# First transposed weight block made on TensorE, first gate product split, in a fused GELU MLP forward and backward kernel

## The chip, the cores and the metric

The kernel runs on one core of a Trainium2 chip. The metric is the device time of one execution in microseconds. Before the change it is 275.32 us, the median of three runs (275.23, 275.32, 275.83). The profile shown is one more execution, of 275.51 us; the span from its first to its last instruction is 273.7 us, and TensorE's granted clock was 1.0.

A core has five engines that run their own instruction streams side by side: TensorE (PE; PEld is its weight load), VectorE (DVE), ScalarE (ACT), GpSimd (POOL) and SyncE (SP). Transfers between HBM and on-chip memory are issued on the queues of SP, ACT and POOL. Matrix products write to PSUM, in eight banks of 128 x 512 f32.

## The reference

An MLP with a tanh-approximated GELU, and its gradients, with S = 2048 rows, D = 448, F = 1792, all in bf16:

```python
def _fwd_reference(x, w1, b1, w2, b2):
    h = jnp.einsum("bsd,df->bsf", x, w1) + b1
    h = _gelu(h)
    return jnp.einsum("bsf,fd->bsd", h, w2) + b2

_out, _vjp = jax.vjp(_f, x, w1, b1, w2, b2)
_grads = _vjp(grad_out)      # for x, w1, b1, w2, b2
```

With u = x w1 + b1 and h = gelu(u), the kernel must give out = h w2 + b2, and from q = grad_out w2^T and gh = gelu'(u) * q the five gradients: gh w1^T, x^T gh, the column sums of gh, h^T grad_out and the column sums of grad_out.

## The kernel before, in words

Everything is held transposed: u, h, q and gh have the feature dimension F on the partitions, 128 at a time. S is cut into 4 blocks of 512 rows and F into 7 pairs of 128-row tiles, which makes 28 steps `g`, one block after the other. One step computes, for a pair of F tiles and a block of 512 rows:

- u (`M1` and `rest`, L239 and L249): 6 products over full 128 rows of D and 2 over the last 64, into one double-bank PSUM tile `u`.
- q (`M4` and `rest`, L258 and L252): the same number, into the double-bank tile `q`. Their stationary operand is `w2T_sb`, w2 transposed.
- On ACT (`act_first`): u to `V` with its bias (L285, twice), its square `A` (L286) and h by the GELU table (L287); later the tanh (L357).
- On DVE: the cubic (L354), the slope (L361 to L364) and the gate (L375), which multiplies the slope with q and writes gh. `V`, `A` and the cubic have one buffer each, `u` and `q` one PSUM tile each.
- Beside it TensorE runs "pieces" (L406): single products of 448 columns that add up earlier h tiles times w2 (out, kind "o") or earlier gh tiles times w1^T (kind "g"). A unit of 14 pieces has one of the four banks of `psum_a`, which are handed out in turn.

The order on every engine is the order in which the program is written; nothing reorders it. Each step `g` writes the remainder of u of the next step, q of its own, the gate, the ACT chain of the next step, the pieces, and M1 of the step after the next.

The start is written out by hand, because the inputs arrive piece by piece. The loads go on SP's queue in the order of L189 to L218 (three small ones on ACT's). x, grad_out and w2 are loaded with a transposing DMA (`load_x`, `load_g`, `load_w2T`), 256 or 512 rows at a time; w1, and w2's rows for the pieces (`load_w2`), with plain ones. The first step is cut into two halves of 256 rows, `r`:

- `keep_warm` (L279): products whose result nobody reads, eight at first on zeros, later on loaded data.
- `first_products` (L297, L300): u of step 0. Its halves go to two banks of `psum_a` and to a tile of the pool that holds `q`.
- `first_chain` (L311 to L336): on each half the ACT and DVE chain up to the finished slope.
- `M1(1)` and `rest(1, None)`: u of step 1.
- Three products of `keep_warm`, then `first_q` (L271): q of step 0, by halves in one double-bank tile, eight products a half, with one more of `keep_warm` between. It reads rows 0 to 256 of `w2T_sb`, and both halves of grad_out's first block.
- In the loop, `dve_gate(0)` (L371): two gates, one for each half; then the pieces of step 0, two products for each of four out units.

After the 28 steps the remaining pieces run, then the gradients of w1 (L569, L577) and of w2 (L588). Two sums over the partitions are made on POOL (L544, L555).

Of the kernel before, what the change touches and what calls it, by code (L numbers as in the profile page):

```python
# [7 lines left out]

# [10 lines left out]
def kernel(  # L19
# [15 lines left out]
    nc = tc.nc  # L35
# [29 lines left out]
    psum_g = ctx.enter_context(tc.tile_pool(name="psum_g", bufs=1, space=bass.MemoryType.PSUM))  # L65
    psum_a = ctx.enter_context(tc.tile_pool(name="psum_a", bufs=4, space=bass.MemoryType.PSUM))

# [120 lines left out]
    nc.vector.memset(w128[:], 1.0 / P)  # L188
    load_x(0, 0, HB)  # L189
# [4 lines left out]
    nc.scalar.activation(out=T_flat[0:1, SB + 2:SB + 3], in_=ones, func=ACT.Gelu_apprx_tanh)  # L194
    load_w1(nc.sync, 256, 512)
    load_g(0, 0, HB)
    load_w2T(0, 256)
    load_g(0, HB, SB)
    load_w2(0, 2)
# [61 lines left out]
    def first_q():  # L261


        q = psum_g.tile([P, 2, SB], F32, name="q")
        g_of[0] = q
        for r in range(2):
            rs = slice(r * HB, (r + 1) * HB)
            for kt in (KF, *range(KF)):
                ps = slice(0, DL if kt == KF else P)
                for h in range(2):  # L270
                    nc.tensor.matmul(q[:, r, h * HB:(h + 1) * HB], lhsT=w2T_sb[ps, kt, cols(0, h)], rhs=gq(0)[ps, kt, rs],  # L271
                                     start=(kt == KF and h == 0), stop=(kt == KF - 1),
                                     tile_position=(0, 0) if kt == KF else None, skip_group_check=True)
            if r == 0:
                keep_warm(1, w1_sb[:, 1, 0:P], xq(0)[:, 1, :])
# [13 lines left out]
    def first_products():  # L289

        ub = psum_g.tile([P, 2, SB], F32, name="q")
        u_of[0] = [[psum_a.tile([P, SB], F32, name="acc")[:, 0:HB] for h in range(2)], [ub[:, h, 0:HB] for h in range(2)]]
        for r in range(2):
# [8 lines left out]
            if r == 0:  # L302
                keep_warm(1, warm[:, 0:P], warm)

    def first_chain():
# [27 lines left out]

        def times(r):
# [7 lines left out]
        copy(1)  # L342
        square(1)
        tanh(0)
        gelu(1)
        slope(0)
# [4 lines left out]
        times(1)  # L351

# [13 lines left out]
    def dve_gate(g):  # L366
        q = g_of.pop(g)
        if g == 0:
            for r in range(2):
                rs = slice(r * HB, (r + 1) * HB)  # L370
                nc.vector.scalar_tensor_tensor(out=ghT(g)[:, :, rs], in0=t_of(g)[:, :, rs], scalar=1.0,  # L371
                                               in1=q[:, r, :].rearrange("p (h s) -> p h s", h=2),
                                               op0=ALU.add, op1=ALU.mult)
        else:
# [253 lines left out]
```

## Time and profile before

| what | value |
|---|---|
| median of three runs | 275.32 us |
| the profiled execution | 275.51 us |
| its span | 273.7 us |
| TensorE busy | 267.9 us (98%) |
| DVE busy | 191.1 us (70%) |
| ACT busy | 144.1 us (53%) |
| POOL busy | 53.5 us (20%) |
| from 0 to 7.4 us: PE, DVE, ACT busy | 5.89, 2.16, 2.80 us |
| from 7.4 to 14.3 us | 6.38, 5.80, 6.01 us |
| from 14.3 to 48.4 us | 33.53, 33.24, 28.36 us |
| from 48.4 to 270 us | 221.59, 149.90, 106.42 us |

A row such as `13.14 1.28 DVE L371 ... x2 [0.77 <-PE q L271]` gives the start and the duration in us, the engine, the line of the kernel, and in brackets how long the engine stood idle before it and what ended that. In the chain of work, each piece is what the next one waited for; SPq is the issue of transfers on SP's queue. Rows of the form `c <- a, b` name the tile that is written and the ones that are read: `w2T_g` is w2 transposed, `w_gw` is w2's rows, `w_x` is w1, `xg_h` holds x and grad_out transposed.

### The profile page before, as it was taken

The numbers are of one execution on the slowest core, as the hardware profiler recorded it, in microseconds if no ns is written. First come the engines' busy times: TensorE is split into PE (matmuls) and PEld (weight loads), VectorE is DVE, ScalarE is ACT, GpSimd is POOL, SyncE is SP. The second block draws the span as 40 slices with busy tenths as digits, with TensorE's granted clock in tenths as the row PEclk, the third lists the DMA queues.
The fourth block names the chain that finished last, engine by engine and source line by source line (L and its number), as shares of the span: only waits on it lengthen the run. The fifth ranks groups of instructions, "written<-read, shape, count | busy, mean of one in ns | idle before, by whom it ended". The sixth has DMA issues, their size and how long they took to land.

```text
span 273.7 us, 3611 instructions
## 1 busy us (share of the span) xinstructions
PE 267.9 (98%) x1407; PEld 124.7 (46%) x1407; DVE 191.1 (70%) x229; ACT 144.1 (53%) x191; POOL 53.5 (20%) x59
## 2 busy tenths in 40 slices
PE   7999999999999999999999999999999999999995
PEld 3444434444444344444444445554445555555552
DVE  2799999999999999999888871149999970000000
ACT  3968879788988778887777740011111221112111
POOL 0000002830301503033031137111700029300000
PEclk9999999999999999999999999999999999999999
DMA  7999999999579927255534339999999931101111
GB/s 158 197 278 236 153 208 180 305 155 315 125 169 220 251 58 149 37 154 124 137 111 79 110 103 217 273 359 243 174 235 244 240 101 57 44 9 50 50 51 36
DMA packets 101533, 43.78 MB, mean 160 GB/s; under 512 B 90092, under 2 KB 98156, under 8 KB 101516
## 3 DMA queue, kind: packets, MB, share of 16 engines
q1 hardware_dynamic: 94432, 26.91, 52.8%
q0 software_dynamic: 4512, 14.69, 17.1%
q10 hardware_dynamic: 2572, 1.95, 2.3%
q8 instruction: 11, 0.18, 0.3%
q14 instruction: 6, 0.05, 0.1%
HBM read 7.00 MB, written 14.23 MB: 78 GB/s over the span
## 4 chain that ended last, share of the span: by engine, by line
PE 82%; DVE 12%; SPq 2%; DMA 2%; ACT 0%; issue 0%; DVEq 0%
PE acc L406 27%; PE acc L588 16%; PE acc L569 13%; PE q L258 10%; PE u L239 9%; PE u L249 4%; DVE T L361 3%; DVE Bt L354 3%; DVE ghT_h L375 3%; PE acc L577 2%; DMA w2T_g<-in_w_dram 2%; DVE T L364 2%; SPq L145 1%; DVE T L362 1%; PE q L271 1%; DVE T L363 1%
## 5 line engine op out<-in xcount | busy, mean ns | idle before, releaser
L406 PE MATMUL acc<-w_gw,hT_h 128*128 128x448 bf16 x224 | 46.3, 353 | 0.0
L406 PE MATMUL acc<-w1T_gw,ghT_h 128*128 128x448 bf16 x224 | 45.1, 353 | 0.0
L285 ACT ACTIVATE VA<-u,b_col 128x512 f32<-128x512 f32 x54 | 33.9, 679 | 13.3 <-PE u L249 13.3
L239 PE MATMUL u<-xg_h,w_x 128*128 128x512 bf16 x162 | 39.4, 379 | 0.7 <-ACT VA L285 0.6
L258 PE MATMUL q<-xg_h,w2T_g 128*128 128x512 bf16 x162 | 39.7, 381 | 0.0
L375 DVE SCALAR_TENSOR_TENSOR ghT_h<-T,q 128x1024 bf16<-128x1024 bf16 x27 | 33.0, 1220 | 7.9 <-PE q L258 6.6
L569 PE MATMUL acc<-gh_nat,w_x 128*128 128x512 bf16 (+1 forms) x192 | 36.7, 353 | 0.0
L357 ACT ACTIVATE T<-Bt 128x1024 bf16<-128x1024 f32 x27 | 28.5, 1057 | 14.6 <-DVE Bt L354 14.5
L361 DVE SCALAR_TENSOR_TENSOR T<-VA,hT_h 128x1024 bf16<-128x1024 f32 x27 | 33.1, 1227 | 0.0
L354 DVE SCALAR_TENSOR_TENSOR Bt<-VA 128x1024 f32<-128x1024 f32 x27 | 32.9, 1219 | 0.0
L406 PEld LDWEIGHTS <-hT_h 128*128 128x128 bf16 x224 | 21.9, 98 | 21.4
L406 PEld LDWEIGHTS <-ghT_h 128*128 128x128 bf16 x224 | 21.9, 98 | 20.9
L554 DVE TENSOR_TENSOR VA<-VA,gh_nat 128x1792 f32<-128x1792 f32 x14 | 30.0, 2142 | 0.5
L286 ACT ACTIVATE VA<-VA 128x1024 f32<-128x1024 f32 x27 | 28.5, 1057 | 0.9
L287 ACT ACTIVATE hT_h<-VA 128x1024 bf16<-128x1024 f32 x27 | 28.1, 1040 | 0.0
L569 PEld LDWEIGHTS <-w_x 128*128 128x128 bf16 x192 | 18.7, 98 | 17.8 <-issue 0.4
L258 PEld LDWEIGHTS <-w2T_g 128*128 128x128 bf16 x162 | 13.6, 97 | 24.2 <-issue 11.4
L239 PEld LDWEIGHTS <-w_x 128*128 128x128 bf16 x162 | 15.8, 98 | 18.7 <-issue 0.8
L590 ACT CAST w_gw<-acc 128x448 bf16<-128x448 f32 x13 | 6.9, 532 | 32.6 <-PE acc L588 32.6
L571 ACT CAST w1T_gw<-acc 128x512 bf16<-128x512 f32 (+1 forms) x12 | 6.3, 532 | 30.1 <-PE acc L569 27.4
L379 POOL DMA_DIRECT2D hT_dram<-hT_h x28 | 20.4, 729 | 0.1
L420 ACT CAST io_g<-acc 128x448 bf16<-128x448 f32 x16 | 8.3, 520 | 22.6 <-PE acc L406 22.6
(74 smaller groups left out, 241.0 us busy)
## 6 DMA issues: line engine op xcount, KB each, us to landing
hT_dram<-hT_h POOLq DMA_DIRECT2D x28, 256.0 KB, 4.2
out_dram<-io_o POOLq DMA_DIRECT2D x8, 224.0 KB, 4.3
out_dram<-io_g POOLq DMA_DIRECT2D x8, 224.0 KB, 3.4
w_x<-in_x_dram POOLq DMA_DIRECT2D x1, 1344.0 KB, 10.9
w2T_g<-in_grad_out_dram POOLq DMA_DIRECT2D x1, 1344.0 KB, 14.2
out_dram<-w_gw SPq DMA_DIRECT2D x4, 336.0 KB, 2.4
w_x<-in_w_dram SPq DMA_DIRECT2D x2, 384.0 KB, 4.5
out_dram<-w1T_gw ACTq DMA_DIRECT2D x2, 384.0 KB, 4.3
```

The lines of the kernel that those rows point to most:

```text
L239: nc.tensor.matmul(u_of[g][h], lhsT=w1_sb[:, 1 + kt, cols(g, h)], rhs=xq(g // NPAIR)[:, 1 + kt, :], start=(kt == 0), stop=False, skip_grou ...
L258: nc.tensor.matmul(g_of[g][:, h, :], lhsT=w2T_sb[:, kt, cols(g, h)], rhs=gq(g // NPAIR)[:, kt, :], start=False, stop=(kt == KF - 1), skip_ ...
L285: nc.scalar.activation(out=V_of(g)[:, h, :], in_=u[h], func=ACT.Identity, bias=b1_col[:, ft:ft + 1])
L286: nc.scalar.activation(out=A_of(g), in_=V_of(g), func=ACT.Square, scale=math.sqrt(3.0 * GELU_C * GELU_A))
L354: nc.vector.scalar_tensor_tensor(out=B_of(g), in0=A_of(g), scalar=3.0 * GELU_C, in1=V_of(g), op0=ALU.add, op1=ALU.mult)
L357: nc.scalar.activation(out=t_of(g), in_=B_of(g), func=ACT.Tanh, scale=-1.0 / 3.0)
L361: nc.vector.scalar_tensor_tensor(out=p_of(g), in0=A_of(g), scalar=GELU_C, in1=hT(g), op0=ALU.add, op1=ALU.mult)
L375: nc.vector.scalar_tensor_tensor(out=ghT(g), in0=t_of(g), scalar=1.0, in1=q[:], op0=ALU.add, op1=ALU.mult)
L406: nc.tensor.matmul(self.ps[:, 0:D], lhsT=lhsT, rhs=rhs, start=(ft == 0), stop=(ft == NF - 1 and not bias))
L554: nc.vector.tensor_tensor(out=gsb_v, in0=gsb_v, in1=gh_rows(st, 0, NF), op=ALU.add)
L569: nc.tensor.matmul(psv, lhsT=x_all[:, st, kt * P:(kt + 1) * P], rhs=gh_rows(st, a0, a1), start=(st == 0), stop=(st == NS - 1))
L588: nc.tensor.matmul(ps[:, 0:D], lhsT=h_blk[ft][:, st, :], rhs=g_all[:, st, :], start=(st == 0), stop=(st == NS - 1))
```

## The change

- w2's first 256 rows are no longer loaded with a transposing DMA for `w2T_sb`. Their plain load, `load_w2(0, 2)`, which served only the pieces, moves up on SP's queue: from behind grad_out's two halves to directly behind x's, ahead of w1's second part.
- An identity of 128 x 128 is made on POOL (`make_identity`: a clear and an `affine_select`, before which the compiled program loads code for POOL; a further code load stands, as before the change, ahead of the sum at L544).
- `turn_w2`: eight products of w2's rows with the identity, each 128 columns, into two banks, behind `first_products` and ahead of `M1(1)`. `turned(i)`: two ACT copies of 128 x 512 from PSUM into `w2T_sb`, one behind ACT's copy of half 1, one behind half 1's GELU, within `first_chain`.
- u's second half and q of step 0 have tiles of one bank for each half (`psum_h`), in a pool that is closed after the start, and whose banks `q` of the later steps takes over.
- `first_q` runs in two parts: blocks 0 and 1 of D for both halves, then four of the pieces of step 0 (two each of the first two out units), then blocks 2 and 3. Both gates stand behind it. The other four pieces of step 0 remain where they were.
- The four products of `keep_warm` around `first_q` are gone.
- `first_chain` stands behind `M1(1)` and `rest(1, None)` in the text; on ACT and DVE its order changes only by the two copies.

```diff
@@ -5,6 +5,7 @@
 import concourse.tile as tile
 from concourse import bass_isa, bass_utils, mybir
 from concourse._compat import with_exitstack
+from concourse.masks import make_identity
 
 ACT = mybir.ActivationFunctionType
 ALU = mybir.AluOpType
@@ -62,8 +63,10 @@
     iop = ctx.enter_context(tc.tile_pool(name="iop", bufs=2))
     dram = ctx.enter_context(tc.tile_pool(name="dram", bufs=1, space=bass.MemoryType.DRAM))
     psum_u = ctx.enter_context(tc.tile_pool(name="psum_u", bufs=1, space=bass.MemoryType.PSUM))
-    psum_g = ctx.enter_context(tc.tile_pool(name="psum_g", bufs=1, space=bass.MemoryType.PSUM))
     psum_a = ctx.enter_context(tc.tile_pool(name="psum_a", bufs=4, space=bass.MemoryType.PSUM))
+
+    first = ExitStack()
+    psum_h = first.enter_context(tc.tile_pool(name="psum_h", bufs=1, space=bass.MemoryType.PSUM))
 
     hT_dram = dram.tile([F, S], BF16, name="hT_dram")
     hT_dram_v = hT_dram.rearrange("(ft p) s -> p ft s", p=P)
@@ -186,17 +189,18 @@
     nc.vector.memset(ones, 1.0)
     nc.vector.memset(b1_rows, 0.0)
     nc.vector.memset(w128[:], 1.0 / P)
+    ident = T_flat[:, 6 * SB:6 * SB + P]
+    make_identity(nc, ident)
     load_x(0, 0, HB)
     load_x(0, HB, SB)
     nc.scalar.dma_start(out=w1_sb[:, 1:KD, 0:256], in_=w1[DL:D, 0:256].rearrange("(k p) f -> p k f", p=P))
     nc.scalar.dma_start(out=b1_rows[0:NF, :], in_=b1.rearrange("(t p) -> t p", p=P))
     nc.scalar.dma_start(out=w1_sb[DL:P, 0, 0:256], in_=w1[0:DL, 0:256])
     nc.scalar.activation(out=T_flat[0:1, SB + 2:SB + 3], in_=ones, func=ACT.Gelu_apprx_tanh)
+    load_w2(0, 2)
     load_w1(nc.sync, 256, 512)
     load_g(0, 0, HB)
-    load_w2T(0, 256)
     load_g(0, HB, SB)
-    load_w2(0, 2)
     load_w1(nc.sync, 512, 768)
     load_w2T(256, 512)
     load_w2(2, 4)
@@ -258,21 +262,20 @@
                 nc.tensor.matmul(g_of[g][:, h, :], lhsT=w2T_sb[:, kt, cols(g, h)], rhs=gq(g // NPAIR)[:, kt, :],
                                  start=False, stop=(kt == KF - 1), skip_group_check=True)
 
-    def first_q():
-
-
-        q = psum_g.tile([P, 2, SB], F32, name="q")
-        g_of[0] = q
+    def first_q(kts):
+
+
         for r in range(2):
             rs = slice(r * HB, (r + 1) * HB)
-            for kt in (KF, *range(KF)):
+            if kts[0] == 0:
+                g_of.setdefault(0, []).append(psum_h.tile([P, SB], F32, name="h%d" % r))
+            q = g_of[0][r]
+            for kt in kts:
                 ps = slice(0, DL if kt == KF else P)
                 for h in range(2):
-                    nc.tensor.matmul(q[:, r, h * HB:(h + 1) * HB], lhsT=w2T_sb[ps, kt, cols(0, h)], rhs=gq(0)[ps, kt, rs],
-                                     start=(kt == KF and h == 0), stop=(kt == KF - 1),
+                    nc.tensor.matmul(q[:, h * HB:(h + 1) * HB], lhsT=w2T_sb[ps, kt, cols(0, h)], rhs=gq(0)[ps, kt, rs],
+                                     start=(kt == 0 and h == 0), stop=(kt == KF),
                                      tile_position=(0, 0) if kt == KF else None, skip_group_check=True)
-            if r == 0:
-                keep_warm(1, w1_sb[:, 1, 0:P], xq(0)[:, 1, :])
 
     def keep_warm(n, weights, moving):
         for i in range(n):
@@ -288,8 +291,7 @@
 
     def first_products():
 
-        ub = psum_g.tile([P, 2, SB], F32, name="q")
-        u_of[0] = [[psum_a.tile([P, SB], F32, name="acc")[:, 0:HB] for h in range(2)], [ub[:, h, 0:HB] for h in range(2)]]
+        u_of[0] = [[t[:, 0:HB] for t in ua], [psum_h.tile([P, SB], F32, name="h%d" % h)[:, 0:HB] for h in range(2)]]
         for r in range(2):
             rs = slice(r * HB, (r + 1) * HB)
             for h in range(2):
@@ -302,6 +304,18 @@
             if r == 0:
                 keep_warm(1, warm[:, 0:P], warm)
 
+    def turn_w2():
+
+        for kt in range(KD):
+            n = DL if kt == KF else P
+            for h in range(2):
+                o = (2 * (kt % 2) + h) * P
+                nc.tensor.matmul((ta, pw)[kt // 2][0:n, o:o + P], lhsT=w2_sb[:, h, kt * P:kt * P + n], rhs=ident,
+                                 start=True, stop=True)
+
+    def turned(i):
+        nc.scalar.copy(out=w2T_sb[:, 2 * i:2 * i + 2, 0:2 * P], in_=(ta, pw)[i].rearrange("p (k f) -> p k f", k=2))
+
     def first_chain():
 
         V, A, Bt, t, p, h0 = V_of(0), A_of(0), B_of(0), t_of(0), p_of(0), hT(0)
@@ -330,6 +344,10 @@
             nc.vector.scalar_tensor_tensor(out=p[:, :, R[r]], in0=A[:, :, R[r]], scalar=GELU_C, in1=h0[:, :, R[r]],
                                            op0=ALU.add, op1=ALU.mult)
             nc.vector.tensor_scalar(out=p[:, :, R[r]], in0=p[:, :, R[r]], scalar1=-0.5, scalar2=None, op0=ALU.add)
+
+        def gate(r):
+            nc.vector.scalar_tensor_tensor(out=ghT(0)[:, :, R[r]], in0=t[:, :, R[r]], scalar=1.0,
+                                           in1=g_of[0][r].rearrange("p (h s) -> p h s", h=2), op0=ALU.add, op1=ALU.mult)
 
         def times(r):
             nc.vector.tensor_scalar(out=t[:, :, R[r]], in0=t[:, :, R[r]], scalar1=1.0, scalar2=None, op0=ALU.add)
@@ -340,15 +358,22 @@
         gelu(0)
         cubic(0)
         copy(1)
+        turned(0)
         square(1)
         tanh(0)
         gelu(1)
+        turned(1)
         slope(0)
         cubic(1)
         tanh(1)
         times(0)
         slope(1)
         times(1)
+        first_q((0, 1))
+        run_pieces([U["o", 0, j] for j in (0, 0, 1, 1)])
+        first_q((2, KF))
+        gate(0)
+        gate(1)
 
     def dve_first(g):
         nc.vector.scalar_tensor_tensor(out=B_of(g), in0=A_of(g), scalar=3.0 * GELU_C, in1=V_of(g), op0=ALU.add, op1=ALU.mult)
@@ -365,14 +390,7 @@
 
     def dve_gate(g):
         q = g_of.pop(g)
-        if g == 0:
-            for r in range(2):
-                rs = slice(r * HB, (r + 1) * HB)
-                nc.vector.scalar_tensor_tensor(out=ghT(g)[:, :, rs], in0=t_of(g)[:, :, rs], scalar=1.0,
-                                               in1=q[:, r, :].rearrange("p (h s) -> p h s", h=2),
-                                               op0=ALU.add, op1=ALU.mult)
-        else:
-            nc.vector.scalar_tensor_tensor(out=ghT(g), in0=t_of(g), scalar=1.0, in1=q[:], op0=ALU.add, op1=ALU.mult)
+        nc.vector.scalar_tensor_tensor(out=ghT(g), in0=t_of(g), scalar=1.0, in1=q[:], op0=ALU.add, op1=ALU.mult)
 
     def store_h(g):
         b, c = blk(g)
@@ -457,6 +475,8 @@
             turns.setdefault(at, []).append((b, c0, c1))
     stored = 0
 
+    ua = [psum_a.tile([P, SB], F32, name="acc") for _ in range(2)]
+    ta = psum_a.tile([P, SB], F32, name="acc")
     pw = psum_a.tile([P, SB], F32, name="acc")
     keep_warm(8, warm[:, 0:P], warm)
 
@@ -464,24 +484,25 @@
         nc.vector.transpose(out=b1_turned[32 * i:32 * (i + 1), :], in_=b1_rows[:, 32 * i:32 * (i + 1)])
     nc.vector.tensor_copy(out=b1_col[:], in_=b1_turned[:, 0:NF])
     first_products()
-    first_chain()
+    turn_w2()
     M1(1)
     rest(1, None)
-
-    keep_warm(3, w1_sb[:, 1, 0:P], xq(0)[:, 1, :])
-    first_q()
+    first_chain()
+    first.close()
+    psum_g = ctx.enter_context(tc.tile_pool(name="psum_g", bufs=1, space=bass.MemoryType.PSUM))
     for g in range(NSTEP):
         b, c = blk(g)
         pieces = [U[k] for k in seq[b] for _ in range(NF)]
         n = len(pieces)
         own = pieces[n * c // NPAIR:n * (c + 1) // NPAIR]
-        grown = [U[k] for k in grow[b] for _ in range(2)]
+        grown = [U[k] for k in (grow[b] if g > 0 else grow[b][2:]) for _ in range(2)]
         nxt = g + 1 if g + 1 < NSTEP else None
         if g > 0:
             rest(nxt, g)
             M4(g)
         flush(False)
-        dve_gate(g)
+        if g > 0:
+            dve_gate(g)
         if nxt is not None:
             act_first(nxt)
         flush(True)
```

The helper that is called, outside the kernel:

```python
def make_identity(nc, identity, nomemset=False):
    sq1, sq2 = identity.shape
    ...
    nc.gpsimd.memset(identity, 0.0)
    nc.gpsimd.affine_select(out=identity, in_=identity, compare_op=mybir.AluOpType.not_equal,
                            fill=1.0, base=0, pattern=[[-1, sq]], channel_multiplier=1)
```

## The prediction

> **What bounds the kernel now.** I read the page first, then the chain that ended last in order of time, then the start instruction by instruction. The page says that TensorE is busy nearly everywhere, and that DVE still holds an eighth of the chain.
>
> ```profile
> PE 267.9 (98%) x1407; PEld 124.7 (46%) x1407; DVE 191.1 (70%) x229; ACT 144.1 (53%) x191; POOL 53.5 (20%) x59
> ...
> PE 82%; DVE 12%; SPq 2%; DMA 2%; ACT 0%; issue 0%; DVEq 0%
> ```
>
> The chain in order of time says where DVE's share lies (start, duration, what):
>
> ```profile
> 4.80 1.30 SPq L145
> 6.15 4.46 DMA w2T_g<-in_w_dram
> 10.65 1.15 PE q L271 x8
> 12.02 1.10 PE q L271 x8
> 13.14 1.28 DVE ghT_h L371 x2
> 14.42 1.14 DVE Bt L354
> ...
> 47.25 0.43 DVE T L362
> 47.69 0.68 ACT VA L285
> 48.41 1.46 PE u L239 x6
> ```
>
> From 6.15 the end waits for w2's first transposed load (landed 10.61), then for the two halves of the first q, then for DVE. DVE repeats one step every 5.07 us (its L354 starts at 14.34, 19.42, 24.49, 29.56) against TensorE's 4.75 (L239 at 14.48, 19.23, 23.98), up to 47.7. At 48.41 TensorE, idle for 0.58 us before, takes the chain over and keeps it to the end. So a time saved before 14.34 on DVE is kept; a time saved on TensorE there is not.
>
> The start in the timeline (start, duration, engine, line):
>
> ```profile
> 7.37 1.47 PE L239 MATMUL u<-xg_h,w_x 128*128 128x512 bf16 x6
> ...
> 9.31 0.82 PE L279 MATMUL acc<-xg_h,w_x 128*128 128x512 bf16 x3
> ...
> 11.94 0.42 DVE L336 TENSOR_TENSOR T<-T 128x512 bf16<-128x512 bf16 x1
> ...
> 11.99 1.06 ACT L286 ACTIVATE VA<-VA 128x1024 f32<-128x1024 f32 x1
> ...
> 12.97 1.67 PE L406 MATMUL acc<-w_gw,hT_h 128*128 128x448 bf16 x8
> ...
> 13.14 1.28 DVE L371 SCALAR_TENSOR_TENSOR ghT_h<-T,q 128x512 bf16<-128x512 bf16 x2 [0.77 <-PE q L271]
> ...
> 14.34 1.22 DVE L354 SCALAR_TENSOR_TENSOR Bt<-VA 128x1024 f32<-128x1024 f32 x1
> ```
>
> DVE is ready for the first gate at 12.37 and waits 0.77 us for q, for both halves, since they are one tile. L354 also needs ACT's square L286 (ends 13.05). So 0.77 is nearly all that the edit can win.
>
> **SP's queue.** One transpose (1.30 us to issue) goes, and the 0.58 us load of w2's rows moves from 8.94 to 3.56, ahead of w1's second part. So w1's two loads issue at 4.19 and 4.82 (0.63 later), grad's halves at 5.43 (before 4.80) and 6.78 (before 7.49), and all behind them some 1.4 us sooner. With the latencies of the same loads from the DMA view: w2's rows, 3.56 plus 4.0 (their own) or 3.8 (w1's in that place): 7.4, up to 7.56. w1: 4.19 + 3.8 = 7.99, its remainder 4.82 + 3.4 = 8.22. Grad: 5.43 + 4.2 = 9.63 and 6.78 + 4.1 = 10.88, or 11.24 with the 4.46 of the slowest transpose there. The later loads covered themselves before and come sooner.
>
> **TensorE.** The first products end at about 7.3 as before. Eight products of 128 columns with the identity follow, which no row shows. Their weight loads are 98 ns each, 8 x 0.098 = 0.78; the ends are 0.43 (half the 0.107 spacing of 256-column products) and 0.86 (all of it). I take 0.8, near the loads: 7.4 to 8.2. Queued behind them are M1(1) and its remainder, 7.37 to 9.31 before, 1.94 us: now 8.2 to 10.14. Without the wait for w1 at 7.99 to 8.22 nothing could start much sooner, so a shorter turn wins nothing. The four removed warming products (0.21 each) stood in idle time and count as nothing; without their cover TensorE just idles for some tenths.
>
> Then first_q((0, 1)): half 0 at 10.14 to 10.57 (4 x 0.107); half 1 waits for grad's second half, 10.88, and ends at 11.31. Four out products, 4 x 0.187 (eight spaced over 12.97 to 14.48): 12.07. Then first_q((2, KF)): eight took 10.65 to 11.64 before, with the change to 64 rows, so 0.50 a half: half 0 is issued by 12.57 and its gate can start 0.17 later (12.97 to 13.14 before), at 12.74; half 1 at 13.07 + 0.17 = 13.24.
>
> **DVE.** Gates stand 0.60 apart (13.14, 13.74, L354 at 14.34). Gate 0 at 12.74, gate 1 at 13.34, L354 at 13.94: 0.40 sooner than before. Separate tiles are worth what gate 0 gains; without them gate 0 would wait for 13.24 and L354 would start at 14.44.
>
> **ACT.** Two copies of 128x512 from PSUM join, 0.53 each by the CAST rows of L571. The first starts at 8.07, behind the copy of half 1, and fills the idle 0.55 us before the square at 8.62. The second moves tanh(1) from 10.20 to 10.73 and the square of step 1 to 12.52 to 13.58. tanh(1) is wanted by DVE at 11.62, done at 11.34; the square by L354 at 13.94. Both copies are thus hidden, the second with 0.36 us to spare; without that cover its 0.53 would go onto L354.
>
> **POOL.** It has to make the identity: a clear (0.17 by DVE's 128x128 memset, 0.56 by POOL's own 64x256 copy), a code load that the select needs, and the select (0.56 by the copy). The one code load in the trace stands between these two:
>
> ```profile
> 186.21 0.73 POOL L426 DMA_DIRECT2D out_dram<-io_g  x1 [4.57 <-ACT io_g L420]
> 191.87 4.48 POOL L544 PARTITION_ALL_REDUCE T<-Bt  x1 [4.93 <-DVE Bt L543]
> ```
>
> It had from 186.94 on, and the reduction started 0.2 us after DVE's last sum (191.67), so there it cost between 0 and 4.93. The identity is then ready between 0.85 + 0.17 + 0.56 = 1.6 and 0.85 + 0.56 + 4.93 + 0.56 = 6.9, where it is wanted at 7.4: no wait, and no gain below that. I take the upper end, but it is weak: code of the same kind could have been left from the execution before, and then the row prices no load at all. A second load, before the reduction at 191.87, comes with it; its result is only stored (196.64), over 70 us from the end.
>
> The Trainium skill (GPSIMD Engine Reference, section Instruction dispatch) says that the first call of a freshly loaded GpSimd routine pays about 6 us, measured 5.95, with no instruction in the profile. By that figure the identity would be ready at 0.85 + 0.17 + 5.95 + 0.56 = 7.53, 0.13 late, which leaves the sum unchanged; the trace, with at most 4.93 in sight, neither shows nor excludes it.
>
> **Sum.** -0.40 us on L354, kept through DVE's steps to 48.4, since TensorE runs ahead of DVE in all of them. The profiled execution took 275.51 (span 273.7), 0.19 above the median 275.32: 275.1 against its own, 274.9 against the median. From the bounds: everything best, L354 is held by the square at 13.58, -0.76; grad's half at 11.24, 14.30, -0.04.
>
> **Rivals.**
> *The identity is late.* The eight products stand in TensorE's queue ahead of M1(1) and all of first_q, and the first copy stands on ACT ahead of the square of half 1. For: the code load is new at the start, the DMA engines are nine tenths busy from 2 us on, and the only row may not price it. Against: 4.93 bounds it in a stretch as busy. TensorE has 0.31 us to spare (10.57 to 10.88), ACT 0.36; beyond that each microsecond goes onto L354. At 8.1 us the gain is gone; at 8.7 it is slower by 0.2%; an identity at 9.3 gives 275.32 - 0.40 + (1.9 - 0.31) = 276.5.
> *The whole wait goes.* If grad's half lands by 10.5 and the 64-row change costs little, gates start at about 12.4 and L354 at the square, 13.58: 274.6. For: w2's transposed load is no longer between grad's halves. Against: three plain loads, 448 KB together, now go ahead of both, and grad's first half landed 4.2 after issue behind 224 KB.
> *Only the waited-for load changes.* Grad's second half takes the place of w2's and lands at 11.24 or later: 275.3.
> *The start is saved, and the end does not move,* because TensorE is the next bound. Against: M1(8) is ready 0.58 us before it runs, and TensorE itself starts step 1 sooner here. It would give 275.3 too.
>
> **How the numbers follow.** What a measurement of this kernel can tell is about 0.2%, 0.55 us. The likeliest, part of the wait gone, has 0.34 (0.04 of it beyond -0.55); the whole wait gone 0.24; a late identity 0.28, of which 0.24 over +0.55; grad's half late or the gain absorbed 0.14. That makes faster 0.28, within 0.2% 0.44, slower 0.28. The likeliest alone spans 274.7 to 275.3. The range of eight in ten reaches from the whole wait gone, with its tenth of scatter, 274.5, to an identity near 9.2 us, 276.4.
>
> **What would show it.** L313 should start near 7.4 and wait for DMA, not for POOL; the select should end before 7.4. L276's second group of four should wait for grad's transpose near 10.9. L349 should start near 12.7 and L379 near 13.9, by DVE's own order and not by ACT's square. The steps of 5.07 us should follow unchanged, and TensorE's L243 of step 8 start near 48.0. A row "L313 waits for POOL" over half a microsecond makes the prediction wrong; so does a grad half past 11.3, or a gate that starts before 12.5.

## The result, and the profile after

The changed kernel takes 276.88 us, the median of six runs (276.69 to 276.92), against 275.40 (275.23 to 275.83) for the kernel before: 1.0051 times as long, with a 95% interval of 1.0038 to 1.0064. The forecast was 274.9, with a range from 274.5 to 276.4. The profiled execution took 276.89, with a span of 275.1; the clock of TensorE was 1.0.

The page of the changed kernel, its line of busy times and the chain's share by engine:

```profile
PE 266.6 (97%) x1397; PEld 124.8 (45%) x1411; DVE 191.0 (69%) x229; ACT 145.2 (53%) x193; POOL 54.4 (20%) x61
...
PE 85%; DVE 9%; issue 4%; ACT 1%; POOL 0%; DVEq 0%; POOLq 0%
```

TensorE has 1.3 us less to do than before, ACT 1.1 and POOL 0.9 more, DVE as much. What is new is 4% of "issue", time in which the profile shows nothing that the engine waited for. The chain in order of time (start, duration, what) says where it lies:

```profile
0.76 0.17 POOL T masks.py:197
0.99 7.74 issue
8.73 0.36 POOL T masks.py:199
9.10 0.04 issue
9.14 0.72 PE acc L313 x8
...
13.54 1.20 PE h L276 x8
14.76 0.69 DVE ghT_h L349
15.45 0.53 DVE Bt L379
15.97 0.53 issue
16.50 1.22 DVE T L386
...
39.55 0.45 issue
40.00 1.23 DVE ghT_h L393
```

Before, this chain began on SP's queue and led through the transposed load of w2. Now it begins on POOL: 7.74 us between the clear and the select of the identity, and everything on TensorE up to the gates hangs behind it. Another piece of "issue", 0.45 us at 39.55, also has no counterpart before. (The piece at 15.97 costs nothing: it lies within L379, and L386 begins 1.14 behind L379's start, where L361 began 1.13 behind L354's.)

The timeline of the changed kernel has the same from the engines' side, engine by engine (start, duration, engine, line, what; in brackets the idle time before it and what ended that):

```profile
0.73 0.20 POOL masks.py:197 MEMSET T<- 128x128 bf16 x1 [0.29 <-POOLq L633]
8.73 0.35 POOL masks.py:199 TENSOR_SCALAR_AFFINE_SELECT T<-T 128x128 bf16<-128x128 bf16 x1 [7.80 <-issue]
...
7.42 0.10 PEld L313 LDWEIGHTS <-w_gw 128*128 128x128 bf16 x1 [0.43 <-DMA w_gw<-in_w_dram]
9.14 0.72 PE L313 MATMUL acc<-T,w_gw 128*128 128x128 bf16 x8 [1.87 <-POOL T masks.py:199]
9.80 1.47 PE L243 MATMUL u<-xg_h,w_x 128*128 128x512 bf16 x6
...
11.73 1.05 PE L276 MATMUL h<-xg_h,w2T_g 128*128 128x256 bf16 x8
12.62 0.92 PE L424 MATMUL acc<-w_gw,hT_h 128*128 128x448 bf16 x4
13.37 1.35 PE L276 MATMUL h<-xg_h,w2T_g 128*128 128x256 bf16 x8
...
9.56 0.59 ACT L317 CAST w2T_g<-acc 128x512 bf16<-128x512 f32 x1 [1.47 <-PE acc L313]
...
10.71 0.69 DVE L340 SCALAR_TENSOR_TENSOR Bt<-VA 128x512 f32<-128x512 f32 x1 [1.45 <-ACT VA L330]
...
14.11 1.33 DVE L349 SCALAR_TENSOR_TENSOR ghT_h<-T,h 128x512 bf16<-128x512 bf16 x2 [0.45 <-PE h L276]
15.36 1.22 DVE L379 SCALAR_TENSOR_TENSOR Bt<-VA 128x1024 f32<-128x1024 f32 x1
...
40.00 1.22 DVE L393 SCALAR_TENSOR_TENSOR ghT_h<-T,q 128x1024 bf16<-128x1024 bf16 x1 [0.51 <-DVE T L389]
...
49.73 1.46 PE L243 MATMUL u<-xg_h,w_x 128*128 128x512 bf16 x6 [0.58 <-ACT VA L288]
```

The select ends at 9.08, and the products that turn w2's rows (L313, "the turn" from here on) begin at 9.14. Their weights, w2's rows, are there at 7.42, so TensorE waits for POOL alone from then on. This is the sign that the prediction named, L313 waiting for POOL by more than half a microsecond. L379, the cubic of step 1 right behind the two gates (L354 before; the expectations call it the gate's last product), begins at 15.36 instead of 14.34, 1.02 later. From there DVE repeats its step of 5.07 us, except for one stop ahead of its sixth gate at 40.00: 0.51 idle, where there is 0.1 before. The fifth gate is 0.90 later than before (34.52 against 33.62, since one step of the kernel before took 5.20), the sixth 1.31 (40.00 against 38.69). TensorE's L243 of step 8, where the chain before went over to TensorE, begins at 49.73 instead of 48.41 (+1.32), and the end is 1.38 later.

The select waited for code to be loaded. A second load stands ahead of the first sum over the partitions, where it holds nobody up:

```profile
187.52 0.73 POOL L444 DMA_DIRECT2D out_dram<-io_g  x1 [4.57 <-ACT io_g L438]
...
194.31 4.67 POOL L565 PARTITION_ALL_REDUCE T<-Bt  x1 [6.06 <-DVE VA L573]
```

POOL was free at 188.25 and DVE's last partial sum ended at 192.23, two microseconds ahead of this start. So here the load shows its length, 6.06 us from the moment that POOL was free; before, the same instruction began 0.2 us behind DVE's last sum.

### The profile page after: what moved, and what is told of

It reads as the page before. It is cut to its first block, busy times and chain, and to the rows that moved or that the text cites. A ratio compares the mean times of both kernels' runs of the same rounds, so it can differ in the third digit from the quotient of the medians.

```text
span 275.1 us, 3612 instructions
## 1 busy us (share of the span) xinstructions
PE 266.6 (97%) x1397; PEld 124.8 (45%) x1411; DVE 191.0 (69%) x229; ACT 145.2 (53%) x193; POOL 54.4 (20%) x61
## 4 chain that ended last, share of the span: by engine, by line
PE 85%; DVE 9%; issue 4%; ACT 1%; POOL 0%; DVEq 0%; POOLq 0%
PE acc L424 28%; PE acc L609 15%; PE acc L590 13%; PE q L262 11%; PE u L243 10%; PE u L253 4%; PE acc L598 2%; DVE ghT_h L393 2%; DVE T L386 2%; DVE Bt L379 2%; DVE T L389 1%; PE h L276 1%; DVE T L387 1%; DVE T L388 1%; PE q L256 0%
## 5 line engine op out<-in xcount | busy, mean ns | idle before, releaser
L243 PE MATMUL u<-xg_h,w_x 128*128 128x512 bf16 x149 | 38.4, 379 | 1.2 <-ACT VA L288 0.6
L382 ACT ACTIVATE T<-Bt 128x1024 bf16<-128x1024 f32 x27 | 28.5, 1057 | 14.0 <-DVE Bt L379 13.9
L386 DVE SCALAR_TENSOR_TENSOR T<-VA,hT_h 128x1024 bf16<-128x1024 f32 x27 | 32.9, 1219 | 0.0
L379 DVE SCALAR_TENSOR_TENSOR Bt<-VA 128x1024 f32<-128x1024 f32 x27 | 32.9, 1218 | 0.0
L243 PEld LDWEIGHTS <-w_x 128*128 128x128 bf16 x162 | 15.7, 98 | 18.4 <-issue 0.8
```

The lines of the kernel that those rows point to most:

```text
L243: nc.tensor.matmul(u_of[g][h], lhsT=w1_sb[:, 1 + kt, cols(g, h)], rhs=xq(g // NPAIR)[:, 1 + kt, :], start=(kt == 0), stop=False, skip_grou ...
L379: nc.vector.scalar_tensor_tensor(out=B_of(g), in0=A_of(g), scalar=3.0 * GELU_C, in1=V_of(g), op0=ALU.add, op1=ALU.mult)
L382: nc.scalar.activation(out=t_of(g), in_=B_of(g), func=ACT.Tanh, scale=-1.0 / 3.0)
L386: nc.vector.scalar_tensor_tensor(out=p_of(g), in0=A_of(g), scalar=GELU_C, in1=hT(g), op0=ALU.add, op1=ALU.mult)
```

## The experiments

The theory: the late identity moves L379, the stop on DVE adds to it, and the rest of the edit is harmless. The rivals: the turn products, the ACT copies or the moved loads cost by themselves; or the code load's traffic disturbs the inputs' loads. The kernels ran in four sets, each set on one chip together with the kernel before.

**No code load, everything else as changed.** The turn products read the matrix of 1/128 that is there anyway, so that no identity is made. (w2T's first 256 columns are then means and not w2's values.)

```diff
-    ident = T_flat[:, 6 * SB:6 * SB + P]
-    make_identity(nc, ident)
+    ident = w128[:]
```

> The changed kernel, but the eight products take the constant tile w128 (cleared by DVE at 1.2 us) in place of the identity, so no code is loaded for POOL; w2T's first 256 columns are then not w2's, and out_1, out_2 and out_3 are wrong in their first rows. Theory (the code load alone makes the change slow): the products start at 7.4 when w2's rows land, half 1 of first_q waits for grad near 10.5 to 10.9, L379 starts at 13.6 to 13.95 (after: 15.36; before: 14.34), and the time is 0.4 to 0.8 us below before, ratio to before about 0.998. Rival (the turn costs time by itself: eight products and two ACT copies ahead of the rest, three plain loads ahead of grad): L379 at 14.4 or later, ratio 1.001 to 1.005.

Measured: 275.33 (before 275.44), ratio 1.0001 [0.9987, 1.0015].

```profile
7.84 0.74 PE L312 MATMUL acc<-w,w_gw 128*128 128x128 bf16 x8
...
14.08 1.22 DVE L378 SCALAR_TENSOR_TENSOR Bt<-VA 128x1024 f32<-128x1024 f32 x1
```

The loss is gone, so the products, the copies and the moved loads cost no more than the edit wins without the wait; but the gain of 0.40 is not there either. (The stop on DVE is gone as well, so this kernel alone does not tell the two apart.)

**The identity alone,** made and read by nobody, in the kernel before.

```diff
+from concourse.masks import make_identity
...
     nc.vector.memset(w128[:], 1.0 / P)
+    make_identity(nc, T_flat[:, 6 * SB:6 * SB + P])
```

> The kernel before, with the identity made at the start and read by nobody. Theory: the select starts at 8.7 again, no engine waits for it, the time is that of before (ratio 0.999 to 1.001), and the sum over the partitions (L544 before) begins about 6 us after POOL's last transfer instead of 4.9. Rival (the load itself disturbs the start through the DMA engines): L354 after 14.5 and ratio above 1.002.

Measured: 275.37, ratio 0.9988 [0.9973, 1.0004]. The two loads are there, and cost nothing where nobody waits:

```profile
8.69 0.28 POOL masks.py:199 TENSOR_SCALAR_AFFINE_SELECT T<-T 128x128 bf16<-128x128 bf16 x1 [7.76 <-issue]
...
193.28 2.89 POOL L546 PARTITION_ALL_REDUCE T<-Bt  x1 [6.39 <-DVE VA L554]
```

So the load's traffic is no cause: where nobody waits for the identity, the time is that of before within what the interval tells.

**The identity without POOL's code:** a row of 255 elements with a single one, written by DVE, and one transfer on POOL's queue that reads it at a shifted start for each partition.

```diff
-    make_identity(nc, ident)
+    spread = T_flat[0:1, 7 * SB:7 * SB + 2 * P]
+    nc.vector.memset(spread, 0.0)
+    nc.vector.memset(spread[:, P - 1:P], 1.0)
+    nc.gpsimd.dma_start(out=ident.rearrange("p (o f) -> p o f", o=1), in_=bass.AP(spread.tensor, spread.offset + P - 1, [[spread.ap[0][0], 1], [-1, P], [1, P]]))
```

> The changed kernel with a right identity that needs no POOL code: DVE writes one row of 255 zeros with a one in the middle, and one transfer on POOL's queue lays it out, each partition one element further. Theory: the transfer is issued at about 1.3 and lands by 5, so the products wait for w2's rows alone (7.4), and the time is that of the stand-in: 0.4 to 0.8 us below before. Rival (the turn costs by itself): slower than before by 0.1 to 0.5%, as with the stand-in.

Measured: 275.38, ratio 0.9997 [0.9988, 1.0006]; the turn begins at 7.81 and the cubic of step 1 (L382 here) at 14.05. The same finding as with the stand-in, with the whole computation in place.

**A dose.** The stand-in again (w2T's first 256 columns are means, as above), ready behind fifteen POOL copies, which need no code load.

```diff
-    ident = w128[:]
+    ident = T_flat[:, 6 * SB:6 * SB + P]
+    nc.gpsimd.memset(T_flat[0:DL, 7 * SB:7 * SB + 2 * P], 0.0)
+    for i in range(15):
+        nc.gpsimd.tensor_copy(out=T_flat[0:DL, 7 * SB + 2 * P:8 * SB], in_=T_flat[0:DL, 7 * SB:7 * SB + 2 * P])
+    nc.gpsimd.memset(ident, 1.0 / P)
```

> The changed kernel with a constant tile in place of the identity (outputs that depend on w2T's first 256 columns are wrong), which POOL clears behind a row of 15 copies of 64x256, so that it is ready at about 7.5 to 8.5 without any code load. Theory (the delay of the products alone counts): with products that start at T, L379 starts at about 15.36 - (9.14 - T), never below 13.6; for T = 8.2 that is 14.4 and a ratio of about 1.001. Rival (the load itself costs, whatever waits for it): ratio 0.998 for any T in this range.

Measured: 275.94 (before 275.35), ratio 1.0024 [1.0014, 1.0034].

```profile
8.05 0.72 PE L316 MATMUL acc<-T,w_gw 128*128 128x128 bf16 x8 [0.56 <-POOL T L196]
...
14.27 1.22 DVE L382 SCALAR_TENSOR_TENSOR Bt<-VA 128x1024 f32<-128x1024 f32 x1
...
38.90 1.22 DVE L396 SCALAR_TENSOR_TENSOR ghT_h<-T,q 128x1024 bf16<-128x1024 bf16 x1 [0.51 <-DVE T L392]
```

The identity's lateness alone sets L379: both the turn and the cubic begin 1.09 us sooner than in the changed kernel. This kernel is slower than before although its L382 is not late: it has the stop on DVE, which the stand-in without POOL's work did not have. The expected ratio of 1.001 left that out.

**The stop.** Counted over all of DVE's instructions that the trace lists, waits included, the wait for a semaphore ahead of the sixth gate is the 63rd in the changed kernel, and the gate the 64th. The test adds one instruction ahead, which changes that place and nothing else.

```diff
     make_identity(nc, ident)
+    nc.vector.memset(T_flat[0:1, 7 * SB:7 * SB + 1], 0.0)
```

> The changed kernel with one more DVE instruction at the start, a 1x1 clear that nobody reads (0.06 us). Both traces of the changed kernel and that of the late turn show DVE stopped for 0.41 us directly behind its 63rd instruction of the profile, which there is the 0.02 us semaphore wait ahead of the sixth gate; in the other four a long instruction stands in that place and nothing is seen. Theory (the stop belongs to the place in DVE's instruction stream): with everything one place later it disappears from the sixth gate, L379 (now one line later) still starts at 15.3 to 15.4, the time falls by 0.3 to 0.4 us against the changed kernel, ratio to before 1.0035 to 1.0045. Rival (it belongs to the sixth gate and to what runs beside it): the stop of 0.4 us stays, ratio 1.005 to 1.006.

Measured: 276.38, ratio 1.0035 [1.0023, 1.0048].

```profile
9.06 0.72 PE L314 MATMUL acc<-T,w_gw 128*128 128x128 bf16 x8 [0.88 <-POOL T masks.py:199]
...
15.28 1.22 DVE L380 SCALAR_TENSOR_TENSOR Bt<-VA 128x1024 f32<-128x1024 f32 x1
...
39.50 1.22 DVE L394 SCALAR_TENSOR_TENSOR ghT_h<-T,q 128x1024 bf16<-128x1024 bf16 x1
```

An instruction more, and the kernel is half a microsecond faster (0.08 of it by an earlier select): the sixth gate has no idle time ahead of it. Of the sixteen traces of this study, the five with a wait in the 63rd place have a gap of 0.45 or 0.46 us behind it, and the eleven others have no gap over 0.05 ahead of any instruction from the 61st to the 65th. That it is the place is shown; why the 64th is a special one is not.

**Which code is loaded when.** The sum over the partitions is put first in the kernel before.

```diff
     nc.vector.memset(w128[:], 1.0 / P)
+    nc.vector.memset(T_flat[:, 6 * SB:6 * SB + P], 0.0)
+    nc.gpsimd.partition_all_reduce(T_flat[:, 7 * SB:7 * SB + P], T_flat[:, 6 * SB:6 * SB + P], channels=P, reduce_op=bass_isa.ReduceOp.add)
```

> The kernel before, with a sum over the partitions of a cleared 128x128 tile as POOL's first work. Its code was the last to be loaded in the execution before this one. If code that is still there is not fetched again, the sum starts by 2 us; if every load is paid, it starts at 6.5 to 9 us, and the gap of 4.93 in the trace of before was a true price with DVE's sum hiding its end. Either way the time stays that of before.

Measured: one time, 275.89 (with the stop, 0.51 at 39.07).

```profile
1.54 1.07 POOL L190 PARTITION_ALL_REDUCE T<-T  x1 [1.10 <-DVE T L189]
```

The sum begins at once, so its code was there already. That the execution before had left it is the nearest reading; who put it there no row shows. In the eleven traces in which no select comes ahead of the first sum, every sum waits for DVE alone. The changed kernel uses two codes: in each of the five traces with the select first, a pair of instructions named MODIFY_POOL_CONFIG stands ahead of the select and another ahead of the first sum, and a load follows both. The kernel with the sum first has one such pair, ahead of that sum, and no load.

**A load without transfers beside it** was to be timed by an identity and a small sum at the end of the kernel before, behind its second sum.

```diff
+from concourse.masks import make_identity
...
+    spare = T_flat[:, F + D:F + D + P]
+    make_identity(nc, spare)
+    nc.gpsimd.partition_all_reduce(b1_col[:, 0:1], b1_col[:, 1:2], channels=P, reduce_op=bass_isa.ReduceOp.add)
```

> The kernel before, with an identity that nobody reads made on POOL behind its last transfer (about 235.5 us), and then a small sum over the partitions of a spare column: two code loads in a stretch where the DMA engines are busy only about one tenth. If traffic at the start made the load long (7.8 us against 6.06 before the sum at 194), both loads take 6 us or less here; if the select's code is simply larger, its load takes 7.7 to 7.8 again and the sum's about 6.

Measured: one time, 275.28, and no load: the select ran at 234.67, 0.08 us behind the clear. The select ran on the sum's code, so the question was not answered, but the next kernel follows from it.

**One code.** The changed kernel with a sum of one column ahead of the identity, so that the select finds its code in place.

```diff
+    spare = T_flat[:, 7 * SB:7 * SB + 2]
+    nc.vector.memset(spare[:, 0:1], 0.0)
+    nc.gpsimd.partition_all_reduce(spare[:, 1:2], spare[:, 0:1], channels=P, reduce_op=bass_isa.ReduceOp.add)
     make_identity(nc, ident)
```

> The changed kernel, with a one-column memset and a one-column sum over the partitions on POOL ahead of the identity, so that all of POOL's work in the program is of the one code that an execution leaves loaded. Theory (the code load is paid only where the code changes, and the late identity is what the change loses by): the sum begins within 2 us of the start, the identity is ready by about 3 us, the turn waits for w2's rows at about 7.4, the gate's last product (L379 of the changed kernel) begins at 13.6 to 14.1 instead of 15.36, DVE's stop at the sixth gate is not there, and the time is 0.1 to 0.6 us under the kernel before (ratio 0.998 to 0.9995). Rival (a load is paid at every start, or what costs is the products with the identity themselves): the select ends after 8 us again and the ratio is 1.003 or more. Rival (a part of the change other than the identity takes the gain): the identity is ready early, but the ratio stays at 1.000 or above.

Measured: 275.20 (before 275.28), ratio 1.0000 [0.9991, 1.0008].

```profile
1.49 0.39 POOL L195 PARTITION_ALL_REDUCE T<-T  x1 [1.04 <-DVE T L194]
...
2.09 0.29 POOL masks.py:199 TENSOR_SCALAR_AFFINE_SELECT T<-T 128x128 bf16<-128x128 bf16 x1
...
6.27 0.54 PE L305 MATMUL acc<-xg_h,w_x 64*128 64x256 bf16 x2
...
8.04 0.74 PE L316 MATMUL acc<-T,w_gw 128*128 128x128 bf16 x8
...
14.28 1.22 DVE L382 SCALAR_TENSOR_TENSOR Bt<-VA 128x1024 f32<-128x1024 f32 x1
```

The identity is ready at 2.38, and the whole loss is gone, 1.7 us against the changed kernel; the added memset on DVE also does away with the stop, which is a part of that. The turn then begins when TensorE comes to it, behind the first products, which are late in this execution (the last of those on x's first half begin at 6.27 here, at 5.56 before). The expected gain is not there: the rival by which the ratio stays at 1.000 is right about the time.

**The split tiles alone,** q's halves and u's second half in tiles of their own and nothing else, twice, on two chips.

```diff
-        q = psum_g.tile([P, 2, SB], F32, name="q")
-        g_of[0] = q
+        g_of[0] = [psum_h.tile([P, SB], F32, name="h%d" % r) for r in range(2)]
...
+            q = g_of[0][r]
...
+    dve_gate(0)
+    first.close()
+    psum_g = ctx.enter_context(tc.tile_pool(name="psum_g", bufs=1, space=bass.MemoryType.PSUM))
```

> The kernel before with one part of the change alone: first q's halves, and the second half of u, in tiles of one bank each; w2T's first block by transposed load as before. By the profile of before, gate 0 then no longer waits for half 1: half 0 ended at 11.80, DVE is free at 12.37, gate 1 follows when half 1 ends (13.11), L354 starts at 13.74 instead of 14.34: 0.6 us faster, ratio 0.998. Rival (the wait was for the transposed load and not for the shared tile): L354 at 14.3, ratio 1.000.

> The kernel before with first q's halves (and u's half beside them) in tiles of their own and nothing else, a second time, on the chip of the two kernels with one code on POOL. Theory (the split is the part that gains): ratio 0.998 to 0.9995 again, and the kernels with one code are no faster than this by more than 0.1%. Rival (the turn of w2T gains by itself once the identity is in time): both kernels with one code are faster than this by 0.1% or more.

Measured: 275.09 (before 275.44), ratio 0.9988 [0.9979, 0.9997]; then 275.04 (before 275.28), 0.9993 [0.9984, 1.0002]. In the first:

```profile
12.30 1.28 DVE L372 SCALAR_TENSOR_TENSOR ghT_h<-T,h 128x512 bf16<-128x512 bf16 x2
13.50 1.22 DVE L355 SCALAR_TENSOR_TENSOR Bt<-VA 128x1024 f32<-128x1024 f32 x1
```

The gate of half 0 starts right behind its slope, 0.84 us sooner than before. The kernel before loses its 0.77 us because both gates wait for both halves; w2's load itself is no hindrance once half 0 may go ahead. The first interval lies below 1, the second reaches just over it.

**No pieces between first_q's parts,** with the identity by a transfer, and then with one code.

```diff
-        run_pieces([U["o", 0, j] for j in (0, 0, 1, 1)])
...
-        grown = [U[k] for k in (grow[b] if g > 0 else grow[b][2:]) for _ in range(2)]
+        grown = [U[k] for k in grow[b] for _ in range(2)]
```

> The identity by a transfer, and the four out products no longer between first_q's parts but all eight behind it. Theory (with the identity on time, the products between are what still holds gate 0): gate 0 starts when DVE is free, 12.3 to 12.4 for a first product at 4.8, L382 at 13.5 to 13.6, held by ACT's square, time 0.6 to 0.8 us below before, and the same as with split tiles alone (ratio 0.998 to 0.999): the turn then adds nothing to the split tiles. Rival (the sooner w2T is worth something by itself): ratio below 0.9975.

> As the kernel with one code on POOL, and out's first eight products all behind first_q, none between its parts. Theory (the pieces between hold gate 0 by some 0.3 us, and gate 1 only waits for the square): the gate's last product begins at 13.5 to 13.7, and the ratio is 0.9975 to 0.999, the same as that of the split tiles alone. Rival (the order of the pieces is worth nothing): within 0.1% of the kernel with one code and the pieces between.

Measured: 275.34, 1.0001 [0.9992, 1.0011] with the transfer (275.29 before); 274.83, 0.9986 [0.9977, 0.9995] with one code. The latter:

```profile
5.57 0.39 PE L305 MATMUL acc<-xg_h,w_x 64*128 64x256 bf16 x2
...
7.44 0.74 PE L316 MATMUL acc<-T,w_gw 128*128 128x128 bf16 x8 [0.18 <-DMA w_gw<-in_w_dram]
...
12.02 1.28 DVE L352 SCALAR_TENSOR_TENSOR ghT_h<-T,h 128x512 bf16<-128x512 bf16 x2
13.41 1.22 DVE L381 SCALAR_TENSOR_TENSOR Bt<-VA 128x1024 f32<-128x1024 f32 x1
```

This is the fastest of all, 0.45 us under the kernel before and 2.1 under the changed one, though no better than the split tiles alone beyond what the intervals tell apart. What the order of the pieces is worth is not settled: leaving them out from between won 0.37 with one code and nothing with the transfer. The two traces show a difference at the start: without the pieces the cubic waits for ACT's square (it ends at 13.38 with one code and L381 begins at 13.41; at 14.13 and 14.16 with the transfer), and in the trace with the transfer the first products on x's second half were late (the last two begin at 7.88, against 6.87).

**The turn late on purpose:** POOL's identity kept, the turn products behind M1(1) and its remainder, both ACT copies behind half 1's GELU, w2's rows behind w1's, no pieces between.

```diff
+    load_w1(nc.sync, 256, 512)
     load_w2(0, 2)
-    load_w1(nc.sync, 256, 512)
...
-    turn_w2()
     M1(1)
     rest(1, None)
+    turn_w2()
```

> POOL's identity and its code load kept, but the eight products behind u of step 1 instead of ahead of it, both ACT copies behind half 1's GELU, w1's second part ahead of w2's rows on SP's queue, all eight out products behind first_q. Theory (only what is queued behind the late identity pays for it): the identity at 9.1 is covered by u of step 1, which ends at 9.3; the products follow at 9.3 to 10.0; L379 at 14.0 to 14.1, held by ACT's square behind two copies; 0.2 to 0.3 us below before, ratio 0.999. Rival (the code load slows whatever comes with it): ratio 1.003 or more.

Measured: 275.96 (before 275.29), ratio 1.0024 [1.0015, 1.0034].

```profile
10.89 2.23 PE L276 MATMUL h<-xg_h,w2T_g 128*128 128x256 bf16 x16 [0.75 <-ACT w2T_g L317]
...
14.12 1.22 DVE L378 SCALAR_TENSOR_TENSOR Bt<-VA 128x1024 f32<-128x1024 f32 x1 [0.28 <-ACT VA L289]
```

M1(1) covers the late identity. First_q then waits for ACT's copies, but the gates are done 0.28 us before L378, which waits for ACT's square, as expected of it, and begins at 14.12, no sooner than with the stand-in. On top comes the stop, which this kernel has too (0.52 at 38.89).

**The changed kernel again,** beside the second set.

> The changed kernel once more, on the chip of the next two runs. Theory: the select starts at 8.7 again, the products at 9.1, L379 at 15.3 to 15.4, ratio to before 1.004 to 1.006. Open besides: DVE's stop of 0.41 us at 39.6 us, in none of the four other traces; if it belongs to this kernel it comes again at the same step, and the time is 0.35 us more than L379's delay; if it was an accident, the ratio is 1.0037.

Measured: 276.91, ratio 1.0061 [1.0048, 1.0074]; the turn at 9.17, L379 at 15.39, the stop of 0.52 at 40.03.

## Why the prediction was wrong

Two relations hold over these traces and carry the account. First, L379 begins 6.22 to 6.24 us behind the turn in each of the seven kernels with the changed kernel's order, whether the turn is late or not. Second, the time of the profiled execution less the start of the cubic of step 1 (L354 before):

| traces | cubic at | time less that |
|---|---|---|
| before; identity alone; quiet loads | 14.34; 14.30; 14.10 | 261.17; 261.18; 261.18 |
| stand-in; by transfer; the same without pieces | 14.08; 14.05; 14.16 | 261.25; 261.22; 261.13 |
| one code; the same without pieces | 14.28; 13.41 | 261.24; 261.25 |
| split tiles, twice | 13.50; 13.65 | 261.31; 261.37 |
| one memset more | 15.28 | 261.10 |
| with the stop: changed, again, dose, late turn, sum first | 15.36; 15.39; 14.27; 14.12; 14.32 | 261.53; 261.52; 261.52; 261.65; 261.57 |

The mean is 261.22 without the stop and 261.56 with it. So what DVE wins or loses before L354 reaches the end nearly whole, as the prediction had it (the rests without the stop differ by up to 0.27, the starts by 1.87), and the stop costs 0.34 by these means. By DVE's steps it costs 0.41: the step into the sixth gate takes 5.48 or 5.49 in the five traces with the stop, 5.07 or 5.08 in the others. The means differ by less, because the step ahead of it takes 5.19 or 5.20 in nine of the eleven traces without the stop but in only two of the five with it, and 5.07 in the rest; why is open.

**POOL, the step that failed.** "I take the upper end": the identity at 6.9, from a row with at most 4.93 for the code load. Measured: 9.08. That row priced no load. The kernel before uses one code, which is there at the start (a sum at 1.54 finds it), and its 4.93 us were a wait for DVE; what stands ahead of L544 in the program loads nothing there. The prediction had named this as its row's weakness and still took the row. A real load held POOL for 7.80 at the start (7.76 with the identity alone), and for 6.06 and 6.39 ahead of the later sum. The Trainium skill (GPSIMD Engine Reference, section Instruction dispatch) gives about 6 us, 5.95 measured, for the first call of freshly loaded code. The shortest load here, 6.06, agrees with it; the ones at the start are some 1.8 us longer, and where the code is in place there is none. What makes the first longer is open. The DMA engines are nine tenths busy there, but they are no less busy during the later, shorter load of the same trace (mean busy share 0.88 from 0.90 to 8.70, full from 188.2 to 194.3), so their being busy does not tell the two apart.

**The late identity,** the rival with 0.28, is what happened, and its slope of one for one is what the dose showed. Its rule, 13.94 plus the lateness less 0.31 to spare, gives 13.94 + 1.74 - 0.31 = 15.37 for L379, where 15.36 was measured. That it fits to the hundredth is luck: two errors cancel. The path from the turn to L379 is 6.22 and not 6.54: the eight products take 0.66 in TensorE's order, not 0.8, and the first part of first_q 0.89, not 1.17, since nothing waited for grad's second half; the second part and the gates take 0.12 more than forecast. And with no wait for grad there was no 0.31 to spare. (The prediction's chances also count the whole late identity, 0.28, as slower, though 0.04 of it was to lie within 0.55 us; slower adds up to 0.24 and within to 0.48.)

**The time for that** would be 275.32 - 0.40 + 1.43 = 276.35. The stop, which nothing in the profile before announced, adds 0.34. The remaining 0.19 is the step from the profiled execution's 275.51 to the median: "275.1 against its own, 274.9 against the median". By the second relation a run of 275.32 has its L354 at 14.10, not at 14.34; the two kernels with the same start order bear that out, with 14.30 in a run of 275.48 and 14.10 in one of 275.28. The profiled execution was above the median because of the very wait that the edit works on (0.77 there, 0.33 in the run of 275.28), so the 0.19 was subtracted twice. 276.35 + 0.34 + 0.19 = 276.88, the measured median; the fit to the hundredth is no proof, since the 0.34 is a difference of means that scatter by more than 0.1. Read from the two profiled executions alone, the loss of 1.38 is 1.02 at L379, less 0.13 for the one longer step of the kernel before, plus 0.41 for the stop, with 0.08 left over.

**The gain of 0.40** is corrected by the same point. The forecast place, 13.94, was near enough for an identity on time: the kernel with one code has a median of 275.20, and 275.20 - 261.22 = 13.98 (in the three traces the cubic begins at 14.05, 14.08 and 14.28). This too is two errors that cancel: the path is 6.24 and not 6.54, but the turn begins at 7.81 to 8.04 and not at 7.4, since TensorE is not free sooner. The profile before happened to have the soonest end of the first products of all sixteen traces (the last two begin at 6.85; 6.87 to 7.88 in the others). And the kernel before stands at about 14.1 in the median and not at 14.34, so the medians gain 0.06 to 0.11 (275.44 to 275.33 and 275.38, 275.28 to 275.20), which the intervals do not tell from nothing.

**What held.** SP's queue: w2's rows landed by 7.42 in the changed kernel, and by 7.44 where the turn waits for them in the one kernel that has everything else early (7.4 forecast). The ACT copies are hidden where the identity is on time; in the changed kernel the first of them held DVE for 1.45, but TensorE's way was the longer one by 0.45. "Separate tiles are worth what gate 0 gains", 0.50 by the forecast, was about right: by themselves they move L354 by 0.69 and 0.84 against the profile before, which was late, and win 0.24 and 0.35 in the medians. "The whole wait goes" (13.58, 274.6) comes to 13.41 and 274.83 with one code and no pieces between; the split tiles alone come near it, with 13.50 and 13.65. "The end does not move" is refuted by the table, and so is "only the waited-for load changes": no group of first_q waited for grad's second half in the changed kernel.

## What to carry to other kernels

In these traces a GpSimd instruction whose code was not the one in place cost 6 to 8 us, which no row of the kernel with one code shows, and a program that uses two codes paid it in every execution: look at which code is in place at the start, and let the start use that one. A wait that is priced from one profiled execution should be set against the median before it is counted as a gain, since that execution's excess may lie in the same wait. Of an edit with several parts the smallest can hold what there is to gain: here the split tiles alone won 0.24 and 0.35 us, and no kernel with the turn beat them beyond what the intervals tell apart.

## What the runs showed of the hardware

- A real code load of GpSimd: POOL stands idle for 7.68 to 7.99 us at the start in five traces, and for 6.06 to 7.07 ahead of the later sum in the same five. There is none where the code is in place (a sum begins at 1.54 and at 1.49), and then a sum over one column takes 0.39 us and the select begins 0.21 behind it.
- A stop of 0.45 us on DVE when the 63rd instruction that the trace lists is a bare wait for a semaphore: in five traces of five, and in none of the other eleven. The step that holds it is 0.41 longer.
- The first products scatter from execution to execution: the last two on x's first half begin between 5.56 and 6.50 in sixteen traces. The mean is 5.94 in the ten traces with w2's rows loaded sooner and 5.93 in the six without, so no delay by the moved loads is to be seen.
